# Two-stage softmax attention and a squared-ReLU MLP on one core: batch 0 in pieces, the first softmax transposed on VectorE, pv as small products for two quads

## Chip, core and metric

The program runs on one core of a Trainium2 chip. The time is the device time of one execution in microseconds; the time before is the median of three runs, 251.08 us (250.28 to 251.39). A core has five engines with a queue of instructions each, which they work off in order: TensorE (PE, matrix products; PEld is its loading of weights), VectorE (DVE), ScalarE (ACT), GpSimd (POOL) and SyncE (SP). They wait for one another by semaphores. Sixteen DMA engines move data between device memory (HBM) and the on-chip SBUF; SP's and ACT's DMAs go through hardware queues, POOL's through a software queue that can also convert f32 to bf16 on the way. PE writes to PSUM, eight banks of 2 KB per partition; ACT and DVE read it.

## What is computed

Shapes: 8 batches, 8 heads, 576 positions, head dimension 64; 32 packing queries p per head; the MLP has 512 inputs, 2048 hidden units and 512 outputs, on 4608 rows.

```python
def sm_attn(qq, kk, vv):
    s = scale * np.matmul(qq, kk.transpose(0, 1, 3, 2))
    s = s - np.max(s, axis=-1, keepdims=True)
    a = np.exp(s)
    a = a / (np.sum(a, axis=-1, keepdims=True) + 1e-09)
    return np.matmul(a, vv)
p_packed = sm_attn(p, k, v)
attn = sm_attn(q, p_packed, p_packed)
x = attn.transpose(0, 2, 1, 3).reshape(B * S, H * D)
h = x @ w_in
out = np.maximum(h, 0.0) ** 2 @ w_out
```

## The kernel before

Four heads of one batch make a quad (QH = 4), so each batch b has two quads, qd = 0 and 1. Four heads of 32 packing queries fill the 128 partitions. The kernel never forms x: it multiplies the packed result of the first attention by w_in (wp, "w" steps), and layer 1 is that product applied to the second softmax.

The order of all work is written out by hand in the string ORDER; each word is one step, and `run` walks the words, so the words give the order on every engine's queue. Digits name batch and quad, a letter after a colon the engine (v = DVE, a = ACT, p = POOL). The steps, for a quad:

- Lk, Lq, Lv: load k, q, v (`load1`), by POOL's queue, f32 to bf16. k and q lie as 128 partitions of 18 consecutive rows; v as 96 partitions (PS) of 6 rows (J). For batches in PAIRED (2 to 7) the q of quad 1 is loaded with its halves swapped, in two DMAs (`group`).
- kT, qT: DVE transposes in 32x32 blocks. P0, P1: p of batch 0 and 1, cast and transposed on DVE; p_f, their f32 source, is the first DMA of SP, in `setup`.
- s1: scores of p with k (`scores`, 16 products of 32x32 weights a quad), m1 their maximum (DVE), x1 the exponential with its sum (ACT), rd the reciprocal of the sum.
- eT, eo: the exponentials are transposed by PE, six products against the identity, and copied from PSUM (`st_e1T`, `st_e1T_out`). pv: 24 products with v (`st_pv`). pp: times the reciprocal. bd: DVE transpose of pp; pt, po: pp transposed by PE and copied.
- s2: scores of q with the packed result, t2 their transpose out of PSUM by DVE, m2 the maximum per query, sb the subtraction, x2 the exponential, su sum and reciprocal, a2 the scaling, aT the transpose to a2T.
- w0, w1 and W0, W1: the packed result times w_in, 512 of its columns at a time, and the copy of it to SBUF. Wi, Wo: loads of w_in and w_out in four pieces each.

Then, for each batch: h, layer 1 of one block of 128 hidden units (16 blocks) over half of the positions (b.half.block; batch 0 takes both halves in one step); r, the ReLU out of PSUM (ACT or DVE); q with dots, the square, written to gT (DVE). o tt.j: two of the 16 accumulating layer-2 products for the 128 output rows of tile tt; c: the copy of its result, and SP's stores. In time, layer 1 of batch b, layer 2 of the batch before and the attention of the batch after are woven together.

The Z words are products of zeros on PE into ps_idle (Z32 is 32 of them). PSUM is split by stages (STAGES): four banks stay with psa, in pairs, for all of the attention; the other four are first three "spare" banks and one for Z, then two pairs for batch 0's layer 1, then two for o and two "early", then two for o and two for h.

```python
STAGES = ((("spare", 3), ("idle", 1)), (("pair", 2),), (("pso", 2), ("early", 2)), (("psh", 2),))
```

## Time and profile before

| | |
|---|---|
| median of three runs | 251.08 us (250.28 to 251.39) |
| span of the profiled execution, first to last instruction | 248.6 us |
| first layer-1 product (h) begins | 23.15 us |
| first layer-2 product (o) begins | 37.3 us |
| last layer-2 product ends | 243.8 us |
| DMA, HBM read / written | 37.22 MB / 9.44 MB |
| PE's granted clock, mean | 0.995 |

The profile is of one execution. Busy times are the time in which an engine had an instruction at work; instructions of PE overlap, so a matmul's own duration is longer than the distance to the next one. "Releaser" is what ended an engine's wait. The costliest groups of the page (line, engine, operation, output<-input, shapes, count | busy us, mean ns | idle us before it):

```profile
L490 PE MATMUL ps_o<-w_out_bf,gT 128*128 128x512 bf16 x544 | 144.2, 379 | 2.0 <-issue 0.5
L444 ACT ACTIVATE r<-ps_h 128x288 bf16<-128x288 f32 (+1 forms) x181 | 73.1, 426 | 55.9 <-PE ps_h L438 47.5
L438 PE MATMUL ps_h<-a2T,wp 128*128 128x288 bf16 x512 | 91.9, 286 | 1.4 <-ACT r L444 1.4
...
L479 DVE TENSOR_TENSOR gT<-r 128x576 bf16<-128x576 bf16 x128 | 54.7, 448 | 5.2 <-ACT r L444 4.9
```

The first two lines of PE are layer 2 and layer 1; ACT's ReLUs wait for PE (47.5 us in all), not PE for them (1.4 us).

### The profile page before, as it was taken

The numbers are of one execution on the slowest core, as the hardware profiler recorded it, in microseconds if no ns is written. First come the engines' busy times: TensorE is split into PE (matmuls) and PEld (weight loads), VectorE is DVE, ScalarE is ACT, GpSimd is POOL, SyncE is SP. The second block draws the span as 40 slices with busy tenths as digits, with TensorE's granted clock in tenths as the row PEclk, the third lists the DMA queues.
The fourth block names the chain that finished last, engine by engine and source line by source line (L and its number), as shares of the span: only waits on it lengthen the run. The fifth ranks groups of instructions, "written<-read, shape, count | busy, mean of one in ns | idle before, by whom it ended". The sixth has DMA issues, their size and how long they took to land.

```text
span 248.6 us, 6041 instructions
## 1 busy us (share of the span) xinstructions
PE 237.1 (95%) x2415; PEld 132.2 (53%) x2447; DVE 194.2 (78%) x411; ACT 145.7 (59%) x316; POOL 45.8 (18%) x75
## 2 busy tenths in 40 slices
PE   8998899998999999999999999999999999999992
PEld 5655554465556554655456555655555555555540
DVE  1888899978988899979887998898897798644710
ACT  2346784476968748755764658676957555353100
POOL 8329634350401500033000230010000000000000
PEclk9999999999999999999999999999999999999997
DMA  6999999999791992269812794252121213211323
GB/s 112 203 207 205 206 197 209 197 142 259 161 171 64 157 211 45 46 93 187 185 42 45 135 130 122 64 90 56 42 45 42 45 42 82 49 42 44 70 63 82
DMA packets 23358, 28.52 MB, mean 115 GB/s; under 512 B 4257, under 2 KB 14753, under 8 KB 23329
## 3 DMA queue, kind: packets, MB, share of 16 engines
q0 software_dynamic: 16880, 18.55, 47.1%
q1 hardware_dynamic: 6288, 9.44, 15.0%
q8 instruction: 19, 0.31, 0.5%
q10 hardware_dynamic: 160, 0.13, 0.2%
q14 instruction: 11, 0.08, 0.1%
HBM read 37.22 MB, written 9.44 MB: 188 GB/s over the span
## 4 chain that ended last, share of the span: by engine, by line
PE 81%; DMA 10%; issue 2%; DVE 2%; POOL 2%; ACT 1%; SPq 0%; ACTq 0%; POOLq 0%
PE ps_o L490 48%; PE ps_h L438 24%; DMA v_b<-in_v_dram 4%; PE ps_wp L422 3%; PE ps_s L295 3%; DMA w_in_bf<-in_moe_w_in_dram 3%; DMA out_dram<-o_sb 3%; PE ps_e1T L339 1%; PE ps_pv L352 1%; POOL k_b L242 1%; DVE mx L387 1%; POOL d L391 0%; ACT r L444 0%; POOL q_b L242 0%; PE ps_ppT L372 0%
## 5 line engine op out<-in xcount | busy, mean ns | idle before, releaser
L490 PE MATMUL ps_o<-w_out_bf,gT 128*128 128x512 bf16 x544 | 144.2, 379 | 2.0 <-issue 0.5
L444 ACT ACTIVATE r<-ps_h 128x288 bf16<-128x288 f32 (+1 forms) x181 | 73.1, 426 | 55.9 <-PE ps_h L438 47.5
L438 PE MATMUL ps_h<-a2T,wp 128*128 128x288 bf16 x512 | 91.9, 286 | 1.4 <-ACT r L444 1.4
L490 PEld LDWEIGHTS <-gT 128*128 128x128 bf16 x576 | 54.9, 98 | 42.1 <-issue 3.3
L438 PEld LDWEIGHTS <-wp 128*128 128x128 bf16 x512 | 47.4, 98 | 44.4 <-issue 7.7
L479 DVE TENSOR_TENSOR gT<-r 128x576 bf16<-128x576 bf16 x128 | 54.7, 448 | 5.2 <-ACT r L444 4.9
L446 DVE TENSOR_SCALAR r<-ps_h 128x288 bf16<-128x288 f32 (+1 forms) x59 | 28.5, 484 | 20.0 <-PE ps_h L438 18.8
L332 ACT CAST wp<-ps_wp 128x1024 bf16<-128x1024 f32 x29 | 28.9, 1016 | 3.8 <-PE ps_wp L422 3.7
L332 ACT COPY o_sb<-ps_o 128x512 f32<-128x512 f32 x27 | 15.9, 588 | 10.8 <-PE ps_o L490 9.4
L321 ACT ACTIVATE e<-ps_s,nm 128x576 bf16<-128x576 f32 x16 | 11.8, 736 | 13.0 <-DVE nm L316 13.0
L233 POOL DMA_DIRECT2D v_b<-in_v_dram x16 | 11.1, 695 | 44.2 <-PE ps_pv L352 22.5
L279 DVE STREAM_TRANSPOSE kT<-k_b 128x576 uint32<-128x576 uint32 x16 | 15.0, 943 | 5.1 <-DMA k_b<-in_k_dram 5.1
L263 PE MATMUL ps_idle<-nought 128*128 128x288 bf16 x95 | 14.4, 304 | 1.1 <-DVE nought L178 1.1
L383 DVE STREAM_TRANSPOSE s<-ps_s 128x576 f32<-128x576 f32 x16 | 12.0, 767 | 2.4 <-PE ps_s L295 2.4
L401 DVE TENSOR_REDUCE sums<-e 128x18 f32<-128x576 f32 x16 | 11.9, 741 | 1.4 <-ACT e L396 1.3
L242 POOL DMA_DIRECT2D k_b<-in_k_dram x16 | 9.0, 562 | 21.4 <-DVE kT L279 12.5
L422 PE MATMUL ps_wp<-w_in_bf,ppT 64*32 64x512 bf16 x256 | 11.4, 382 | 0.8 <-DMA w_in_bf<-in_moe_w_in_dram 0.7
L316 DVE TENSOR_REDUCE nm<-ps_s 128x1 f32<-128x576 f32 x16 | 11.6, 739 | 0.6 <-PE ps_s L295 0.6
L285 DVE STREAM_TRANSPOSE qT<-q_b 128x576 uint32<-128x576 uint32 x16 | 12.0, 761 | 0.0
L387 DVE TENSOR_REDUCE mx<-s 128x18 f32<-128x576 f32 x16 | 11.9, 743 | 0.1
L396 ACT ACTIVATE e<-d 128x576 f32<-128x576 f32 x16 | 11.0, 685 | 1.6 <-DVE d L391 1.4
L263 PEld LDWEIGHTS <-nought 128*128 128x128 bf16 x95 | 9.2, 103 | 4.9 <-issue 1.2
(47 smaller groups left out, 153.0 us busy)
## 6 DMA issues: line engine op xcount, KB each, us to landing
out_dram<-o_sb SPq DMA_DIRECT2D x70, 128.0 KB, 2.8
k_b<-in_k_dram POOLq DMA_DIRECT2D x16, 288.0 KB, 8.1
v_b<-in_v_dram POOLq DMA_DIRECT2D x16, 288.0 KB, 7.4
q_b<-in_q_dram POOLq DMA_DIRECT2D x10, 288.0 KB, 7.2
w_in_bf<-in_moe_w_in_dram POOLq DMA_DIRECT2D x4, 512.0 KB, 12.5
w_out_bf<-in_moe_w_out_dram POOLq DMA_DIRECT2D x4, 512.0 KB, 13.8
q_b<-in_q_dram POOLq DMA_DIRECT2D x12, 144.0 KB, 3.9
p_b<-in_p_dram POOLq DMA_DIRECT2D x1, 192.0 KB, 11.5
```

The lines of the kernel that those rows point to most:

```text
L263: self.nc.tensor.matmul(ps[:, :HALF], lhsT=self.nought[:, :P], rhs=self.nought, start=True, stop=True)
L279: return self.nc.vector.transpose(t["kT"][:].rearrange("p (j l a) e -> p a j l e", j=J, a=3).bitcast(U32).rearrange("p a j l e -> p a j (l ...
L285: return self.nc.vector.transpose(t["qT"][:].rearrange("p s e -> p (s e)").bitcast(U32), t["q"][:].rearrange("p t d -> p (t d)").bitcast(U32))
L332: engine.copy(out, x)
L383: nc.vector.transpose(s2[:].rearrange("p (a t) i -> p a (t i)", a=2), t["ps_s2"][:, :, :HALF])
L387: self.nc.vector.tensor_reduce(out=t["mx"], in_=t["s2"], op=ALU.max, axis=AX.X)
L422: self.nc.tensor.matmul(ps[NP * h:NP * h + NP, c, :], lhsT=t["ppT"][D * c:D * c + D, NP * g:NP * g + NP], rhs=self.w_in_bf[D * c:D * c + D ...
L438: self.nc.tensor.matmul(ps, lhsT=t["wp"][:, fb // n, fb % n * P:(fb % n + 1) * P], rhs=t["a2T"][:, hf * HALF:(hf + 1) * HALF], start=(qd = ...
L444: engine.activation(r, ps, ACT.Relu)
L446: engine.tensor_scalar_max(r, ps, 0.0)
L479: (engine or self.nc.vector).tensor_tensor(out=out, in0=r, in1=r, op=ALU.mult)
L490: self.nc.tensor.matmul(self.o[tt], lhsT=self.gT[:, fb, a:a + P], rhs=self.w_out_bf[:, fb, :], start=(i == 0), stop=(i == self.NFB - 1))
```

## The change

The new kernel has another ORDER throughout and these changed steps.

- k of batch 0 is loaded as f32 by SP's queue into the still unused last two blocks of gT, and cast to bf16 in two halves, one on DVE and one on ACT (ka, kb). p_f is no longer loaded in `setup` but by the word pf, between the two k's.
- v lies like k and q, 18 rows to a partition. The exponentials of the first softmax are transposed by DVE in 32x32 blocks (eo); PE's transposes and their copies are gone. pv is 18 rounds of products with 32 rows and 32 columns; from batch 1 on both quads run in one step, on different tiles of the array (8 products a round, 144 in all), as do rd, pp, bd, pt, po and s2.
- PAIRED begins with batch 1; q is loaded whole, and v of quad 1 with its halves swapped.
- The second softmax of batch 0 runs in two parts, positions 0 to 319 and 320 to 575 (tA, mA, sA, xA, uA, aA, TA and tB to TB), and so do layer 1, ReLU and square of batch 0 (PARTS).
- w_in is loaded as four quarters of 256 columns and two pieces of 512; wp of batch 0 has two quarter steps (wa, wb) ahead of w1.
- POOL does more of the subtractions (sb), scalings (a2) and some squares of batch 0. Z32 at the start is gone.
- The second stage of PSUM is two banks "x" and two "y" for everything behind the first layer-1 step.

```diff
-PAIRED = range(2, 8)
+PAIRED = range(1, 8)
+PARTS = {False: ((0, HALF), (HALF, S)), True: ((0, 320), (320, S))}
 ORDER = """
-Lk00 Lk01 Lq00 kT00 P0 Z32 s100 kT01 I m100 x100 Z5 s101 m101 x101 Lq01 P1 Z7 eT00 Lv00 eo00:a Lk10 Z10 pv00 rd00
-qT00 rd01 qT01 pp00:v bd00 eT01 kT10 Lv01 Z3 s200 Wi00 Wi01 pt00 eo01:a Lk11 Z5 pv01 s110 pp01:a t200 pt01 Wi10 bd01
...
+Lk00 I pf Lk01 Lq01 Lv00 Lq00 Lv01 kb00:v ka00:a Wi11 P1 P0 Wi01 kT00 Wi10 kb01:a s100 ka01:v Wi00 m100 Wi20 kT01 x100
+qT01 Z15 s101 Wi21 eo00 rd00 m101 Z2 pv00 x101 Lk11 pp00:v qT00 bd00 Z7 pt00 rd01 eo01 s200 Lv11 po00:v pv01 tA00 tB00
+pp01:a mA00 Lk10 bd01 Z5 pt01 mB00 s201 po01:a sA00:v sB00:p tB01 Wo0 xB00 tA01 xA00 mB01 Z10 wb00 Wo2 mA01 Wb00:a
+wb01 uB00 sA01:p uA00 Wb01:a Z4 wa01 Lv10 aB00:v xA01 aA00:v wa00 sB01:p Wa01:a uA01 Wa00:a TA00 aA01:p xB01 TB00 TA01
+Lq10 uB01 Z16 h0.0.0 h0.0.1 r0.0.0:a h0.0.10 r0.0.1:v h0.0.3 aB01:p r0.0.10:a h0.0.8 q0.0.0:v r0.0.3:a h0.0.9 h0.0.2
...
-    STAGES = ((("spare", 3), ("idle", 1)), (("pair", 2),), (("pso", 2), ("early", 2)), (("psh", 2),))
+    STAGES = ((("spare", 3), ("idle", 1)), (("x", 2), ("y", 2)))
...
+    def bank(self, pool, name):
+
+        return self.banks(pool).tile([P, 512], F32, name=name, tag="t")
...
+    def load_w_in(self, n, c):
+        f0, f1 = ((0, 256), (256, 512), (512, 1024))[n]
...
     def load1(self, b, qd, n):
+        s = getattr(self, n)[b, qd * QH:(qd + 1) * QH].rearrange("h (l t) d -> (h l) t d", t=T)
+        x = self.ld.tile([P, T, D], BF16, name=f"{n}_b")
...
+        if (n, b) == ("k", 0):
+
+            f = self.gT[:, self.NFB - 2:, :].rearrange("p f s -> p (f s)").bitcast(F32)[:, qd * T * D:(qd + 1) * T * D]
+            t["f"] = f.rearrange("p (t d) -> p t d", d=D)
+            self.nc.sync.dma_start(t["f"], s)
+        elif n == "v" and self.group(b, qd, 0):
+            n2 = P // 2
+            self.nc.gpsimd.dma_start(x[:n2], s[n2:])
+            self.nc.gpsimd.dma_start(x[n2:], s[:n2])
         else:
+            self.nc.gpsimd.dma_start(x, s)
...
+    def st_cast(self, t, n, engine):
+        x = slice(n * T // 2, (n + 1) * T // 2)
+        self.copy(engine, t["k"][:, x, :], t["f"][:, x, :])
...
-    def st_e1T(self, t, b):
-        ps = self.bank16(b, "ps_e1T")[:PS, :J * P].rearrange("p (j c) -> p j c", c=P)
-        for j in range(J):
-            self.nc.tensor.transpose(ps[:, j, :], t["e1"][:, j * PS:(j + 1) * PS], self.ident)
-        t["ps_e1T"] = ps
-
-    def st_e1T_out(self, t, engine):
-        t["e1T"] = self.tp.tile([PS, J, P], BF16, name="e1T")
-        self.copy(engine, t["e1T"], t["ps_e1T"])
+    def st_e1T(self, t):
+
+        t["e1T"] = self.tp.tile([P, T // 2, NP, 2], BF16, name="e1T")
+        self.nc.vector.transpose(t["e1T"][:].rearrange("p t i e -> p (t i e)").bitcast(U32), t["e1"][:].bitcast(U32))
...
+    def st_pv(self, b, *qds):
+
+        ps = self.bank32(b, "ps_pv", len(qds))
+        for j in range(T):
+            for i, qd in enumerate(qds):
+                t = self.att[b, qd]
+                t["ps_pv"] = ps
+                for h in range(QH):
+                    r, c = NP * self.group(b, qd, h), NP * h
+                    self.nc.tensor.matmul(ps[c:c + NP, i, :D], lhsT=t["e1T"][r:r + NP, j // 2, :, j % 2],
+                                          rhs=t["v"][r:r + NP, j, :], start=(j == 0), stop=(j == T - 1))
...
+    def span(self, hf):
+
+        s0, s1 = (0, S) if hf is None else PARTS[True][hf]
+        return slice(s0 // NP, s1 // NP)
...
+    def st_sub2(self, t, engine, hf=None):
+        x = self.span(hf)
+        d2 = self.new(t, self.tp, "d2", [P, T, NP], F32)
+        n = x.stop - x.start
+        engine.tensor_tensor(out=d2[:, x], in0=t["s2"][:, x], in1=t["mx"][:, x].unsqueeze(2).to_broadcast([P, n, NP]),
+                             op=ALU.subtract)
...
+    WP = {"0": (0, 512), "a": (0, 256), "b": (256, 512), "1": (512, 1024)}
...
+    def step_h(self, engine, b, hf, fb):
+
+        s0, s1 = PARTS[b == 0][hf]
+        ps = self.ph[b, hf, fb] = self.bank("y" if b or fb % 2 else "x", "ps_h")
+        self.layer1(ps[:, :s1 - s0], b, fb, s0, s1)
...
+        elif word == "pf":
+            self.nc.sync.dma_start(self.p_f, self.packed(0, 2 * self.NQ))
```

## The prediction

> **What bounds the kernel now.** I read the engine totals first, then busy time by stretch, then the chain of waits, then the timeline of the first 36 us, then the groups with their shapes kept apart.
>
> ```profile
> span 248.6 us, 6041 instructions
> PE 237.1 (95%) x2415; PEld 132.2 (53%) x2447; DVE 194.2 (78%) x411; ACT 145.7 (59%) x316; POOL 45.8 (18%) x75
> ...
> PE 81%; DMA 10%; issue 2%; DVE 2%; POOL 2%; ACT 1%; SPq 0%; ACTq 0%; POOLq 0%
> ```
>
> TensorE (PE) is busy 95% of the span and carries 81% of the chain. Its own count includes 14.4 us of ps_idle matmuls (the Z words), so the start needs a look of its own.
>
> ```profile
> 23.00:37.70 14.70, 13.43 (x192) 8.00 (x186) 12.60 (x28) 10.83 (x18) 8.18 (x13) 1.00 1.34 202
> 37.70:60.00 22.30, 21.26 (x239) 10.72 (x242) 20.07 (x41) 12.69 (x26) 8.12 (x11) 1.00 1.12 199
> 60.00:235.00 175.00, 173.26 (x1680) 96.63 (x1706) 144.82 (x312) 111.44 (x255) 16.82 (x29) 1.00 0.47 91
> ```
>
> Columns: stretch, its length, then busy PE, weight loads, DVE, ACT, POOL. From 60 us on PE lacks 1.7 us in 175, and 32 of the 576 second-layer matmuls have no record, so it is full. Three places can move the end: when the first layer-1 matmul (ps_h) runs, at 23.15 us; what PE has to do from there to 243.8; and its holes, 2.3 us between 23 and 60 (1.27 + 1.04). The last 4.8 us (copy and store of tile 35) stay. So 23.15 + 220.7 + 4.8 = 248.6. The median of the runs, 251.08, is 2.5 above this span; I carry that over.
>
> **Part 1: less on PE per batch.** Taken away: six transposes a quad (eT) and a pv of 24 products with 96 rows. Added: one pv of 144 products with 32 rows for both quads.
>
> ```profile
> 31.81 0.29 PE ps_pv L352 x24
> ...
> 33.25 0.62 PE ps_s L295 x16
> ```
> ```profile
> 99.18 0.63 PE ps_s L295 x32
> ...
> 130.61 0.67 PE ps_e1T L339 x12
> ```
>
> These are pieces of the chain: start, length, what. One transpose is 0.67/12 = 56 ns; after 23.15 there are 13 quads of six, 4.4 us. A quad's pv is 0.29 us, 14 of them 4.1 us; some pairs stand side by side and share the change of tile shape, and the chain's shares (e1T 1.4%, pv 1.3%) give 6.7 us for both together. I take 8.0. The new pv is 18 rounds of eight. A round's price: today 24 products (last one 193 ns long) fill 0.36 us, (0.36 - 0.19)/23 = 7.3 ns each, 29 ns for a round of four. Does a round of eight cost the same? The scores say so: 16 small products take 0.62 us and 32 take 0.63, because the second quad uses other tiles of the array. So a new pv is 18 x 30 ns and 0.22 us for going into small tiles and out, 0.76 us; 7 times 5.3 us. Net **-2.7 us**. Bounds: rounds at 29 ns and 8.5 us removed, -3.3; the two quads one after the other, 18 x 58 ns, 8.9 us, against 6.7 removed, +2.2. I stay near the scores' row, which is the same form of product.
>
> The Trainium skill, "TensorE: Matmul & The Clock Gate", section "Wait — 56ns, not 53.3ns?", speaks against this part: starts never come closer than about 25 ns. By it a pv would take 3.6 us. The 7.3 ns above disagree; it stays as a rival of small chance.
>
> **Part 2: what moves to VectorE (DVE).** The transposes become 16 DVE instructions like a2T's:
>
> ```profile
> L415 DVE STREAM_TRANSPOSE a2T<-a 128x288 uint32<-128x288 uint32 x16 | 7.0, 457 | 0.2
> L391 POOL TENSOR_TENSOR d<-s,mx 128x576 f32<-128x576 f32 x3 | 3.6, 1191 | 7.6 <-DVE mx L387 7.6
> ```
>
> +7.3 us. The new order also gives DVE 6 more wp copies (7.3), 6 more o_sb copies (4.1), some 23 more relus of 288 (10.4), wider pp (about +1.8) and reciprocals (+1). It takes from it e1T copies (3.9), 11.5 subtractions (8.7), 6.5 scalings (5.2), 5 squares (2.2), smaller relus in batch 0 (0.9) and ppT copies (1.0). Net about +10, DVE 204 us. ACT falls to about 120; POOL gets 32 tensor operations where it had 6, about 37 us. In 60 to 180 us DVE was 87% busy (105 of 120 us), so 5% more makes 92%. On average that hides under PE. But DVE and POOL get in each other's way here:
>
> ```profile
> 42.59 1.26 POOL L391 TENSOR_TENSOR d<-s,mx 128x576 f32<-128x576 f32 x1
> ```
> ```profile
> 42.76 1.77 DVE L479 TENSOR_TENSOR gT<-r 128x576 bf16<-128x576 bf16 x2
> ```
>
> Two squares take 1.77 us instead of 0.90: the first waits until POOL's subtraction ends at 43.85. With four POOL operations a batch (4.7 us of some 27) and 16 squares, 2.8 squares a batch run into one and lose some 0.5 us: 1.4 us, 5%, so DVE stands at 97%. A late square or relu holds the two ps_h banks and then PE. I take **+0.7 us** for all later batches; bounds 0 (each wait falls into slack) and +4 (half of 7 x 1.4 shows).
>
> The Trainium skill, "SBUF — State Buffer", section "Who interferes with whom", makes this a lock: a DVE instruction with two SBUF inputs and a POOL instruction that reads SBUF exclude each other entirely. The trace agrees with 1.77 for 0.90; by that rule each meeting costs the whole rest, as counted.
>
> **Part 3: the start.** Today p_f lands before 3 us, the first scores run at 7.05, the second v lands at 14.4 (seventh transfer of 1.4 us each, saturated), the last w_in piece at 26.8.
>
> ```profile
> 23.15 1.15 PE L438 MATMUL ps_h<-a2T,wp 128*128 128x288 bf16 x8
> ...
> 26.82 0.41 PE L422 MATMUL ps_wp<-w_in_bf,ppT 64*32 64x512 bf16 x7 [0.70 <-DMA w_in_bf<-in_moe_w_in_dram]
> ```
>
> After: both k of batch 0 come as f32 through SP's queue (first issue 0.74, first packet 1.85 as p_f had). A 4,608-byte packet is not shown; stores of 1,024 and 2,048 bytes take 74 and 131 ns, which gives about 270; the cast packet that reads as much takes 192. Eight packets an engine: k00 lands at 4.7 with the 0.6 us to a semaphore (today 5.6). Then on DVE half a cast 0.4 (not shown; between the 0.25 of p_b's 128 elements and the 0.8 of a 576-element scaling), the four p instructions 1.0 (they were half hidden), kT 0.95: scores at 7.1, no gain. The second k shares the engines with POOL's loads. Stores and loads that overlap at 63 to 64.5 us go packet for packet (86 to 94), so 8 x (0.27 + 0.19) us from 5.0: it lands at 9.2. Its cast (ka01) stands on DVE ahead of the first row maximum, which moves from 8.00 to 9.6. Z32 is gone, so Z15 runs unwarmed (the first 32 today take 168 ns each, later ones 123) and holds the second scores to about 12.
>
> From there DVE's queue sets the pace, with durations from today's rows less the 0.07 us by which neighbours overlap: second maximum 12.9 to 13.6, pp 14.1, qT and first bd 14.9, second e1T 15.4, second pv on PE 15.7 to 16.3 (v landed near 13: six transfers instead of seven), second bd 17.05. Then the softmax in pieces of 320 and 256, each at 320/576 or 256/576 of its row: transposes, maxima and the one DVE subtraction to 19.3, sums 20.3, scalings 21.4 with one meeting with POOL, last sum 22.0, POOL's scaling 22.7, transpose 23.1. First ps_h at **23.2: no gain**. The second half, from second bd to ps_h, shrinks from 7.9 us to 6.1, and the later first half eats it. w_in does not bind: four quarters at 1.5 us after v put the first half there by 19, the second by 24. Bounds: 22 (k in 192 ns packets, nothing shared) and 28.5 (p_f's 32 small packets an engine alternate with loads of 192 ns, 6.7 us, and k01 queues behind them).
>
> Part 3b, the ramp. Before PE reaches o0.0 it has 9.3 us of work (32 half-width h 7.85, two wp steps, s11). DVE has 8 relus, 10 squares, a wp copy (1.2), two kT (1.9) and remainders of the softmax, 10 us by slots, and 1.7 for meetings with five POOL squares (not shown; the 1.16 of 576 elements gives 1.0 to 1.3): PE gets there near 35, with 2.6 us of holes plus nothing for w_in, against 2.3 today. **+0.3** (-1 to +3).
>
> **Sum:** 0 - 2.7 + 0.7 + 0.3 = -1.7: span 246.9, time **249.4**. v in one 4,608-byte run per partition, q unswapped and v swapped instead, merged pp, ppT: nothing, as PE is full over them; a pv fetch of 288 instructions at once is the uncovered one (inside the bound of part 1).
>
> **Rivals.** (a) The second k is late: SP's queue gets less than its turn while POOL's loads saturate the engines. For it: the first store of today, issued at 50.6 into such a stretch, landed 7.2 us later, against 2.8 in the median. Against: it alternated evenly at 63 us. Until 10 the unwarmed Z15 covers it, then each microsecond delays ps_h by one; from 11.7 on it eats the whole gain. At the 28.5 bound 249.4 + 5.3 = 254.7; half way 252. (b) DVE with POOL's lock becomes the bound from 40 to 180 us: +4 instead of 0.7, 252.7. Against: at 88% from 60 to 120 us it leaves PE full today. It decides once PE's holes pass 2.4 us. (c) The quads' pv do not overlap: 249.4 + 4 = 253.4. (d) As the skill's 25 ns, 7 x 2.8 us more: 269. (e) The pieces work better than I walk: k early, ps_h at 21.5 to 22, ramp without holes (-2) and DVE covered: 246. For it: from second bd on the chain is shorter by 1.8 us already. (f) The order leaves PE as full as it was and nothing shows: 251.
>
> **Chances.** A measurement tells 0.5%, 1.26 us, from no change: faster is below 249.8, slower above 252.3. Forecast 0.42 (its own range 247.3 to 251.3: faster 0.26, same 0.16); (a) 0.15 slower; (b) 0.12 (slower 0.08, same 0.04); (c) 0.06 and (d) 0.01 slower; (e) 0.22 faster; (f) 0.02 same. Faster 0.48, same 0.22, slower 0.30. Range 245.3 to 253.8: it leaves out the best of (e), the worst of (a), and (d).
>
> **What would show it.** pv of both quads near 0.76 us on PE; no e1T on PE; the DVE wait at ka01 and where k01 lands; the first ps_h at 22 to 25; PE idle under 3 us up to o0.0 and under 1.5 from 60 on; squares of 1 us or more beside POOL operations. I am wrong if ps_h starts before 21.5 or after 25, if pv takes over 1.2 us, or if PE has holes in 60 to 180 us.

## The result, and the profile after

The changed kernel takes 265.39 us (median of 4 runs, 264.28 to 265.94) where the kernel before, run beside it, takes 251.24 (4 runs): ratio 1.0543, 95% interval 1.0483 to 1.0602. It is slower by 14 us; the forecast was 249.4, in a range from 245.3 to 253.8. The profiled execution has a span of 262.5 us at a clock of 1.00, 13.9 more than the 248.6 of before.

The page of the changed kernel, engine totals, the instruction queue among the DMA queues, and the chain by engine:

```profile
span 262.5 us, 7413 instructions
PE 237.1 (90%) x3099; PEld 128.5 (49%) x3099; DVE 210.3 (80%) x445; ACT 124.5 (47%) x280; POOL 73.9 (28%) x102
...
q8 instruction: 24, 0.39, 0.6%
...
PE 65%; DVE 25%; DMA 4%; issue 3%; ACT 1%; SPq 0%; POOL 0%; ACTq 0%; DVEq 0%; POOLq 0%
```

PE's busy time is given as 237.1 us, as before, although its idle products (ps_idle) fell from 14.4 to 9.7 us: the change took nothing off PE. (The records of before lack 32 products, so its true figure is somewhat higher.) DVE carries 25% of the chain where it had 2%, and "issue", time in which nothing in the profile is waited for, 3% (2% before). The packets of PE's instructions (q8, 16,384 bytes each) were 19 before and are 24.

Busy time by stretch, in the stretches shown of before (stretch, length, PE, weight loads, DVE, ACT, POOL, clock, DMA):

```profile
23.00:37.70 14.70, 12.10 (x110) 7.57 (x108) 13.78 (x30) 10.51 (x28) 10.93 (x14) 1.00 1.17 208
37.70:60.00 22.30, 18.77 (x308) 8.46 (x309) 16.85 (x33) 9.24 (x18) 10.11 (x14) 1.00 0.95 148
60.00:235.00 175.00, 171.88 (x2296) 93.28 (x2295) 155.09 (x326) 94.44 (x214) 41.22 (x52) 1.00 0.48 94
```

PE loses in every stretch. DVE's 155.1 us in the third are 89% of it, against 83% before (144.8); POOL has 41 us for 17.

Take the time from each product's start to the next: the usual time of its form is its slot, what is over is a hole. That gives the bill. The first ps_h runs at 26.3 instead of 23.15 us (+3.2). The slots from there on add up to 217.1 instead of 216.4 us (+0.7). Holes from there to 60 us are 7.7 instead of 4.2 (+3.5), and after 60 us 6.3, where before shows none but its 32 unrecorded matmuls (+6.3). Together 13.7 of 13.9. Three kinds of places make it up. The timeline of the start, the rows where an engine waited long:

```profile
7.38 0.23 DVE L208 TENSOR_SCALAR p_b<-p_f 128x128 bf16<-128x128 f32 x1 [2.64 <-DMA p_f<-in_p_dram]
...
10.24 0.46 DVE L338 CAST k_b<-gT 128x576 bf16<-128x576 f32 x1 [1.31 <-DMA gT<-in_k_dram]
...
20.56 0.69 PE L303 MATMUL ps_s<-qT,ppd 32*32 32x320 bf16 x16 [2.27 <-issue]
```

DVE waits 2.64 us for p_f (in this execution; other runs with the same start do not show it, see e1) and 1.31 for the second k; and PE stands 2.27 us in front of the second quad's second scores although their weight load could begin at 18.36. The same kind of stop comes in batch 1; the timeline of PE there:

```profile
44.62 1.34 PE L367 MATMUL ps_pv<-v_b,e1T 32*32 32x64 bf16 x144
45.90 1.90 PE L529 MATMUL ps_o<-w_out_bf,gT 128*128 128x512 bf16 x8
...
48.27 0.56 PE L303 MATMUL ps_s<-qT,ppd 32*32 32x288 bf16 x19
51.08 0.44 PE L303 MATMUL ps_s<-qT,ppd 32*32 32x288 bf16 x13 [2.25 <-issue]
```

pv of both quads takes 1.34 us, not 0.76, and the scores stop after 19 of 32 products. The first sixteen have read all the tiles (qT, ppd of both quads) that the rest read, so no operand can be late there. The third kind, all engines near 193 us:

```profile
192.96 2.09 DVE L518 TENSOR_TENSOR gT<-r 128x576 bf16<-128x576 bf16 x3
...
193.18 1.18 POOL L455 TENSOR_TENSOR a<-e,rs 128x576 bf16<-128x576 f32 x1 [2.62 <-ACT r L496]
...
194.73 0.61 PE L529 MATMUL ps_o<-w_out_bf,gT 128*128 128x512 bf16 x2 [0.78 <-DVE gT L518]
```

Three squares fill 2.09 us instead of some 1.3 while POOL's scaling runs from 193.18 to 194.36, and PE waits 0.78 us for the last. The page's squares take 515 ns each on the mean, 448 before, but the 515 mixes three shapes. Those of 576 elements, the only shape of before, take 489:

```profile
L518 DVE TENSOR_TENSOR gT<-r 128x576 bf16<-128x576 bf16 x112 | 53.0, 489 | 3.1 <-ACT r L496 2.1
```

### The profile page after: what moved, and what is told of

Read it like the earlier page. It is cut to its first block, busy times and chain, and to the rows that moved or that the text cites. A ratio compares the mean times of both kernels' runs of the same rounds, so it can differ in the third digit from the quotient of the medians.

```text
span 262.5 us, 7413 instructions
## 1 busy us (share of the span) xinstructions
PE 237.1 (90%) x3099; PEld 128.5 (49%) x3099; DVE 210.3 (80%) x445; ACT 124.5 (47%) x280; POOL 73.9 (28%) x102
## 4 chain that ended last, share of the span: by engine, by line
PE 65%; DVE 25%; DMA 4%; issue 3%; ACT 1%; SPq 0%; POOL 0%; ACTq 0%; DVEq 0%; POOLq 0%
PE ps_o L529 37%; PE ps_h L491 18%; DVE gT L518 7%; PE ps_s L303 4%; PE ps_pv L367 4%; DMA p_f<-in_p_dram 2%; DVE wp L338 2%; DVE sums L447 2%; DVE mx L429 2%; DVE r L498 2%; DMA out_dram<-o_sb 2%; DVE s L416 2%; PE ps_wp L475 2%; PE ps_idle L267 1%; DVE qT L293 1%
## 5 line engine op out<-in xcount | busy, mean ns | idle before, releaser
L496 ACT ACTIVATE r<-ps_h 128x288 bf16<-128x288 f32 (+2 forms) x172 | 66.2, 412 | 76.4 <-PE ps_h L491 72.8
L491 PE MATMUL ps_h<-a2T,wp 128*128 128x288 bf16 (+2 forms) x512 | 91.5, 287 | 3.6 <-DVE a2T L464 1.4
L491 PEld LDWEIGHTS <-wp 128*128 128x128 bf16 x512 | 48.1, 98 | 50.2 <-issue 11.2
L518 DVE TENSOR_TENSOR gT<-r 128x576 bf16<-128x576 bf16 (+2 forms) x123 | 61.4, 515 | 3.2 <-ACT r L496 2.1
L498 DVE TENSOR_SCALAR r<-ps_h 128x288 bf16<-128x288 f32 (+2 forms) x84 | 37.2, 452 | 13.8 <-PE ps_h L491 12.9
L435 POOL TENSOR_TENSOR d<-s,mx 128x576 f32<-128x576 f32 (+2 forms) x16 | 18.6, 1166 | 56.5 <-DVE mx L429 56.5
L336 ACT CAST wp<-ps_wp 128x1024 bf16<-128x1024 f32 (+1 forms) x25 | 23.2, 955 | 8.9 <-PE ps_wp L475 8.8
L455 POOL TENSOR_TENSOR a<-e,rs 128x576 bf16<-128x576 f32 (+2 forms) x11 | 11.9, 1081 | 14.9 <-DVE rs L449 11.2
L329 ACT ACTIVATE e<-ps_s,nm 128x576 bf16<-128x576 f32 x16 | 11.8, 743 | 4.2 <-DVE nm L324 4.2
L324 DVE TENSOR_REDUCE nm<-ps_s 128x1 f32<-128x576 f32 x16 | 11.7, 748 | 1.3 <-PE ps_s L303 1.3
L441 ACT ACTIVATE e<-d 128x576 f32<-128x576 f32 (+2 forms) x18 | 11.0, 635 | 2.6 <-POOL d L435 2.6
L447 DVE TENSOR_REDUCE sums<-e 128x18 f32<-128x576 f32 (+2 forms) x18 | 11.9, 663 | 0.2 <-ACT e L441 0.2
L429 DVE TENSOR_REDUCE mx<-s 128x18 f32<-128x576 f32 (+2 forms) x18 | 11.6, 660 | 0.0
## 6 DMA issues: line engine op xcount, KB each, us to landing
w_in_bf<-in_moe_w_in_dram POOLq DMA_DIRECT2D x4, 256.0 KB, 11.8
```

The costliest lines, as they stand in the source:

```text
L336: engine.copy(out, x)
L429: self.nc.vector.tensor_reduce(out=mx[:, x], in_=t["s2"][:, x], op=ALU.max, axis=AX.X)
L435: engine.tensor_tensor(out=d2[:, x], in0=t["s2"][:, x], in1=t["mx"][:, x].unsqueeze(2).to_broadcast([P, n, NP]), op=ALU.subtract)
L447: nc.vector.reduce_sum(out=sums[:, x], in_=t["e2"][:, x], axis=AX.X)
L491: self.nc.tensor.matmul(ps, lhsT=t["wp"][:, fb // n, fb % n * P:(fb % n + 1) * P], rhs=t["a2T"][:, s0:s1], start=(qd == 0), stop=(qd == se ...
L496: engine.activation(r, ps, ACT.Relu)
```

## The experiments

The theory I set out to test: (A) PE's instructions come too slowly for the bursts of pv, and pv itself is limited by instructions; (B) POOL's tensor operations shut out DVE's two-input ones. The rivals: DVE's load, the start's transfers, the order of the work. Times of before are 251.4 to 251.7 in these runs.

| run | time, us | ratio to before, 95% interval |
| --- | --- | --- |
| changed kernel | 265.39 | 1.0543 (1.0483 to 1.0602) |
| e1 p_f first | 264.85 | 1.0546 (1.0503 to 1.0589) |
| e2 half of pv | 256.12 | 1.0199 (1.0151 to 1.0246) |
| e3 pv with 32 columns | 262.81 | a single run |
| e4 pv in two halves | 267.15 | 1.0582 (1.0504 to 1.0660) |
| e5 160 instructions more | 271.79 | 1.0774 (1.0703 to 1.0845) |
| e6 p_f first, fewer idle products | 265.31 | 1.0527 (1.0466 to 1.0588) |
| e7 subtractions on DVE | 269.95 | 1.0727 (1.0667 to 1.0788) |
| e8 relus on ACT | 263.55 | 1.0482 (1.0408 to 1.0556) |
| e9 eight POOL operations on DVE | 261.82 | 1.0394 (1.0330 to 1.0459) |
| e10 quads apart, 4 o_sb | 261.72 | 1.0380 (1.0309 to 1.0451) |
| e11 all repairs | 259.52 | 1.0296 (1.0231 to 1.0362) |
| e13 all repairs, relus on ACT | 259.52 | 1.0328 (1.0287 to 1.0369) |
| e16 without 13 subtractions | 262.23 | 1.0397 (1.0342 to 1.0453) |
| e12 before, 24 steps on POOL | 261.46 | 1.0383 (1.0322 to 1.0445) |
| e14 before, no step on POOL | 253.63 | 1.0100 (1.0070 to 1.0131) |
| e15 before, batch 1's steps on DVE | 251.54 | 0.9992 (0.9962 to 1.0022) |

### What a pv product costs, and half of pv

Half of pv:

```diff
-        for j in range(T):
+        for j in range(0, T, 2):
...
-                                        ..., stop=(j == T - 1))
+                                        ..., stop=(j == T - 2))
```

> Only every second round of the pv products is issued (9 of 18), so half of pv is left out; 72 products a batch instead of 144, in batch 0 36 instead of 72 for each quad. Theory (a round of eight costs 64 ns, and the burst of 288 instructions, products and their weight loads, runs PE's instruction supply dry): pv falls from 1.16-1.34 to about 0.65 us for each of 7 batches (-4.2), the stalls put down to issue at 18.4 (2.2 us) and 48.5 (2.4 us) are gone or under 0.5, PE's instruction fetches fall from 24 to about 20; time about 257 to 258. Rival (the two stalls come from something else, a late operand or a full DMA queue): pv falls the same, the two stalls of over 2 us stay; time about 261.5.

Products of 32 columns:

```diff
-    matmul(ps[c:c + NP, i, :D], lhsT=..., rhs=t["v"][r:r + NP, j, :], ...)
+    matmul(ps[c:c + NP, i, :NP], lhsT=..., rhs=t["v"][r:r + NP, j, :NP], ...)
```

> Each pv product streams 32 columns of v instead of 64, so the other half of pv's columns is left out; as many products and weight loads as before. Theory (PE takes in small products and their weight loads at about 4 ns an instruction, 8 ns a product): unchanged, 144 products in 1.16 us or more, 8 ns each. Rival (the array or PSUM limits: the quads' tiles do not overlap, and a product occupies something for its columns): 32 columns take half, about 4 to 5 ns a product, 0.6 to 0.7 us for 144. Time 265 by the first, 261 by the second.

The timeline of e3, PE, pv of batch 1 and the scores behind it:

```profile
43.30 1.32 PE L367 MATMUL ps_pv<-v_b,e1T 32*32 32x32 bf16 x144
...
49.50 0.44 PE L303 MATMUL ps_s<-qT,ppd 32*32 32x288 bf16 x13 [2.01 <-issue]
```

144 products take 1.32 us with half the columns and 1.34 with all: 7.96 and 8.05 ns from start to start. So the columns do not set the price, and neither do the tiles: one quad alone (72 products, four tiles) starts a product every 7.8 to 8.0 ns too. What is common is two instructions a product, a weight load and a matmul, some 4 ns each. Which of the two sets it was not tried. The rows of the weights do not matter either: the pv of before, with 96 rows, has starts 7.2 to 7.7 ns apart. The scores do better than 8 ns only in appearance: eight of them start close together and then wait for 288 columns.

In e2, pv falls to 0.75 us (72 products) as both sides expected, the fetches fall to 19, the stop behind pv of batch 1 is gone and the first ps_h comes at 24.7. The time fell by 9.3 us, to 256.12, a little below the theory's 257 to 258. The profiled execution, 257.73 us, shows a new wait (ACT, then PE):

```profile
61.73 0.58 ACT L336 COPY o_sb<-ps_o 128x512 f32<-128x512 f32 x1 [2.15 <-DMA out_dram<-o_sb]
```
```profile
62.37 0.59 PE L529 MATMUL ps_o<-w_out_bf,gT 128*128 128x512 bf16 x2 [1.81 <-ACT o_sb L336]
```

The fourth o_sb copy must wait until the first store, issued among the loads, has left its buffer. In the changed kernel the stop at 48.5 had covered this: ACT waited 0.41 us there. Between these two profiles, then, the stop of 2.4 us costs only some 0.5 net.

### The stops: a burst, a place, or the supply of instructions

pv in two halves of nine rounds, two PE steps apart (batch 1 shown):

```diff
- o3.0 pv1 o3.1 pp1 Lk21 o1.1 qT10
+ o3.0 pv1 o3.1 Lk21 o1.1 pw1 pp1 qT10
```

> In batches 1 to 7 the pv products are issued in two halves of 9 rounds with two PE steps (0.25 to 0.43 us each) between them; batch 0 is left as it is. Each half goes into and out of small tiles by itself, 7 x 0.19 us more. Theory (the burst outruns the instruction supply): the stall of 2.4 us behind pv of batch 1 is cut to under 1.2, that of 0.6 behind pv of batch 5 goes; time 265.4 - 1.8 + 1.3 = 264.9. Rival (a stall that has nothing to do with the burst): both stay, and the time is 266.7 by the tile changes and a later pp.

It came out as the rival said: the stop in s21 is still there (2.6 us, at 49.0). The packets of the instruction queue tell why. Places were counted in PE's weight loads and matmuls, in order. Packets are 256 instructions long, and the stops fall on places 449 and 1217, three times 256 apart, in e1, e3 and e4 as well as in the changed kernel. In e4 the piece from 961 to 1216 was entered at 44.7 us and run dry at 49.0 all the same: two steps are only 0.9 us. So the next run moves the places instead of the burst:

```diff
- qT01 Z15 s101
+ qT01 Z11 Y84 s101
...
+    def small(self, n):
+        ps = self.banks("idle").tile([P, 512], F32, name="ps_idle")
+        for i in range(n):
+            r = c = NP * (i % 4)
+            self.nc.tensor.matmul(ps[c:c + NP, :NP], lhsT=self.nought[r:r + NP, :NP],
+                                  rhs=self.nought[r:r + NP, :NP], start=True, stop=True)
```

> Z15 is replaced by 11 of its products and 84 tiny ones (32x32 on a diagonal tile), about as long together; every later PE instruction stands 160 places further on. Theory (PE takes its instructions in pieces of 256; a piece is asked for when PE enters the piece before it and is there 2.4 us after its packet starts, 3 to 4 us after the request while the loads fill the DMA engines until about 72 us and about 1 us later on; a stall comes where one piece is run through in less): worked out from the instruction times of the changed kernel with boundaries moved by 160, the stalls at 18.4, 48.5 and 179.6 us are under 0.3, and new ones of 2 to 4 us stand at 66 to 70 (scores and pv of batch 2) and of 0.5 to 2 near 130; first ps_h near 25, time 264 to 267. Rival (these stalls belong to their place: the burst itself, an operand, the DMA engines): the stalls of 2.2 to 2.4 us behind pv01 and behind pv of batch 1 stay where they are, none appears at 66 to 70; time 265.5 to 266.

The timeline of e5, PE, batches 2 and 4:

```profile
68.33 1.32 PE L375 MATMUL ps_pv<-v_b,e1T 32*32 32x64 bf16 x141
71.77 0.21 PE L375 MATMUL ps_pv<-v_b,e1T 32*32 32x64 bf16 x3 [2.12 <-issue]
...
129.20 1.33 PE L375 MATMUL ps_pv<-v_b,e1T 32*32 32x64 bf16 x142
132.95 0.23 PE L375 MATMUL ps_pv<-v_b,e1T 32*32 32x64 bf16 x2 [2.41 <-issue]
```

The stops at 18.4, 48.5 and 179.6 are gone; two new ones stand in the middle of pv, three and two products before its end, where no data can be the reason, at 69.5 and 130.3 as forecast. That settles it: the supply of instructions. Places and packets fit one rule at all of these stops. From the trace's records, us: when PE enters a piece of 256, when the next piece's packet starts, PE's last instruction before the stop (a weight load in the first row, products in the others), its first product after it, and the time from the packet to that.

```
kernel    enters    packet    last     first    packet to first
changed   14.58     18.13     18.4     20.56    2.43
changed   44.99     48.68     48.5     51.08    2.40
e5        68.39     69.17     69.5     71.77    2.60
e5       129.27    130.73    130.3    132.95    2.22
e6        12.77     16.34     17.0     18.75    2.41
```

A piece is asked for when PE enters the one before it; its packet starts 2 to 5 us later while the loads fill the DMA engines (in the changed kernel up to 73 us) and mostly within 1.5 us in the rest of the kernel; 2.2 to 2.6 us after its start PE can use it. The entry is known to about a microsecond only: from 100 us on, seven packets of the changed kernel start 0.2 to 1.3 us before it. A piece with most of a pv in it is run through in less. The Trainium skill, "Runtime: NRT & Kernel Launch", section "Instruction fetch mechanics", has the blocks of 256 and calls the cost of crossing one mostly hidden. The 24 packets of 16,384 bytes agree; that it stays hidden does not: 2.2 to 2.6 us here. The time of e5 was higher than I said, 271.8 for 264 to 267: beside the two stops the wait for o_sb came back (1.84 us at 61.3), and the products of batch 0 took 12 ns. The trace shows one thing more: from 132.2 us, near the end of the stop that begins at 130.3, to 139.0 PE's granted clock is 0.50, and products of 512 columns start 427 ns apart instead of 216. Half of those 6 us, some 3 us, is lost there (an estimate). The changed kernel's own two stops, 2.3 and 2.4 us long, have no such stretch behind them. Nor did the first ps_h come near 25: it is at 26.2, as the second k landed at 11.35 and the stop at 18.4 was not the only thing that held it.

The quads' pv apart, each a burst of 144 instructions, and a fourth o_sb buffer (batch 1 shown):

```diff
- eo11 q0.1.2:p o1.0 x110 ... eo10 Lq20 o3.0 pv1
+ eo11 q0.1.2:p o1.0 pv11 x110 ... eo10 Lq20 o3.0 pv10
...
-        self.op = pool("op", 3)
+        self.op = pool("op", 4)
```

> In batches 1 to 7 each quad's pv is a word of its own, the first one right after its own e1T, the second where pv of both stands now, 1.5 to 4 us later; o_sb gets 4 buffers instead of 3. Theory (a burst of 288 PE instructions runs through a piece of 256 before the next piece is there; and a pair of quads saves nothing, 8.05 ns a product as one quad alone): two bursts of 144 cost 0.74 to 0.76 us each plus 0.19 for another change of tile shape, +1.8 us in all; the stall at 48.5 falls from 2.4 to under 0.8, that at 179.6 goes, and with a fourth o_sb buffer no wait for a store takes its place near 61: time 265.4 + 1.8 - 2.9 = 264.3. Rival (the pieces are late whatever the burst): both stalls stay, 267.2.

The timeline of e10, PE, batch 1:

```profile
42.87 0.75 PE L362 MATMUL ps_pv<-v_b,e1T 32*32 32x64 bf16 x72
43.55 1.90 PE L524 MATMUL ps_o<-w_out_bf,gT 128*128 128x512 bf16 x8
45.38 0.75 PE L362 MATMUL ps_pv<-v_b,e1T 32*32 32x64 bf16 x72
...
48.43 0.79 PE L293 MATMUL ps_s<-qT,ppd 32*32 32x288 bf16 x32
```

All 32 scores run through, nothing waits at 61 or at 179, and the time is 261.72, 3.7 us less than the changed kernel and 2.6 less than I expected; the two edits were not run apart. What is left after 60 us is 5.0 instead of 6.3. Only the stop in batch 0 stays (2.4 us at 18.0): there the bursts follow too closely.

### The start

```diff
- Lk00 I pf Lk01
+ pf Lk00 I Lk01
```

> The p_f transfer is issued ahead of k00 on SP's queue; nothing else changes. Theory (p_f late sets the start): today k00 lands at 4.19 us and DVE then waits 2.64 us for p_f, until 7.38. With p_f first that wait is under 0.3 us, kT of quad 0 starts near 5.7 instead of 7.43 and the first scores run near 6.5 instead of 8.98, Z15 ends that much earlier, and the first ps_h moves from 26.3 to about 24.3; time about 263.4. Rival (the second k, landing at 10.24, and the wait of 1.31 us for it set the start): p_f's move only changes places with k01, the second scores stay at 13.2 us and the first ps_h at 26 or later; time 265.4 +- 0.5.

The rival was nearer. The wait for p_f is gone, but now k00 lands at 6.21 instead of 4.19 us, behind p_f; the first scores run at 8.30 instead of 8.98, the first ps_h at 25.8 instead of 26.3, and the time does not differ from the changed kernel's. The wait of 2.64 us belongs to that one execution: in five runs that leave the start as it is (e7 to e10 and e16) p_f is there with k00, DVE does not wait for it, and the first scores run at 6.6 to 6.9, yet the first ps_h comes at 25.6 to 26.8. What p_f's place does move is the second k: it lands at 9.27 with p_f first, at 10.2 to 11.3 in those five. The PE timeline of e1 shows what holds the second scores here:

```profile
9.38 3.28 PE L267 MATMUL ps_idle<-nought 128*128 128x288 bf16 x15
12.59 0.69 PE L303 MATMUL ps_s<-kT,pT 32*32 32x288 bf16 x16
```

The second scores follow right behind the idle products; their kT was ready at 11.08. So next also `Z15` cut to `Z4`:

> p_f first on SP's queue, and the 15 idle products ahead of the second scores cut to 4. Theory (in the first 13 us the idle products hold the second scores: kT of quad 1 is ready at 11.1 us, the scores of quad 1 run at 12.6 with p_f first and at 13.2 without): the second scores run at 11.2 to 11.4, the second maximum at 12, and the first ps_h comes 1.0 to 1.5 us earlier than the 25.8 of p_f alone, as far as the stall of 2.4 us ahead of the second quad's second scores lets it: 24.4 to 24.8; time about 263.5. Rival (DVE's queue sets the pace, or the colder clock lengthens the scores): the second maximum stays behind qT and e1T on DVE at 12.5 or later and the first ps_h at 25.5; time 265.

The second scores run at 10.4 and the first ps_h at 24.2, a little earlier than expected, as the second k landed at 8.50; the time, 265.3 where 263.5 was expected, does not show it. The stop moved with the 22 instructions that fell away (11 products and their weight loads): it now comes after 11 of the 16 products of s201 instead of ahead of the first, which agrees with the count. Other stops grew (1.0 us at 151.9, in pv of batch 5).

### POOL against DVE

> The 13 subtractions of batches 1 to 7 that run on POOL go to VectorE, as 11.5 of them did before; POOL keeps 19 tensor operations. Theory (POOL's operations shut out DVE's two-input ones; 123 squares now take 515 ns on the mean against 448): the squares fall to about 480, PE's holes after 60 us fall from 6.4 to about 4; time about 263. Rival (DVE is overloaded, and each piece of its work counts): 13 x 0.75 = 9.8 us more on DVE, less 4 us of squares, PE's holes after 60 us grow to 8 or more; time 267.

```diff
- sb11:p  sb21:p  sb20:p  ... (13 words)
+ sb11:v  sb21:v  sb20:v  ...
```

The rival won: the holes after 60 us grow to 11.8. The mean of the squares falls to 497 ns; those of 576 elements fall from 489 to 469.

```diff
- r2.0.0:v  r2.0.10:v  ... (every second of the 54 words of batches 2 to 6)
+ r2.0.0:a  r2.0.10:a  ...
```

> Every second of the 54 relus that DVE does in batches 2 to 6 goes to ScalarE, 27 in all: DVE 12 us less, ACT 11 us more, at the same places in the order. Theory (DVE's load and queue make the holes after 60 us): PE's holes after 60 us fall from 6.4 to 4 or less, time about 263. Rival (lock, instruction supply and single late links make them): the holes stay at 6 to 7; time 265.4 +- 0.7.

DVE falls to 200.9 us, squares stay at 515 ns, and the holes after 60 us stay where they were, most to within 0.02 us (85.0, 162.1, 163.7, 193.8). So DVE's load as a whole is not what makes them; the time is inconclusive.

```diff
- q0.0.5:p  q0.1.0:p  q0.0.3:p  q0.0.7:p  q0.1.2:p  a220:p  sb50:p  a261:p
+ q0.0.5:v  q0.1.0:v  q0.0.3:v  q0.0.7:v  q0.1.2:v  a220:v  sb50:v  a261:v
```

> Eight of POOL's tensor operations go to VectorE: the five squares of batch 0 and the three steps of batches 2, 5 and 6 beside which a square on DVE stood still ahead of a hole on PE (scaling at 83.9, subtraction at 160, scaling at 193.2 us). Theory (POOL's lock makes these holes): a POOL square takes 1.04 to 1.35 us and keeps DVE's squares out for most of it, DVE itself needs 0.45 to 0.5, so DVE gains time although it takes work over; the holes at 30.8 (1.53), 37.3 (0.95), 39.7 (0.59), 85.2 (0.86), 162.1 (0.47), 163.7 (0.59) and 193.7 (0.94), 5.9 us in all, fall to under 2.5; profiled span 259 against 262.5, time about 262. Rival (DVE is simply full there): the holes stay or grow, as they did with the 13 subtractions on DVE; time 266 or more.

The groups of squares with shapes kept apart, the changed kernel, then e9:

```profile
L518 POOL TENSOR_TENSOR gT<-r 128x640 bf16<-128x640 bf16 x3 | 3.9, 1294 | 1.3 <-DVE r L498 1.2
L518 DVE TENSOR_TENSOR gT<-r 128x640 bf16<-128x640 bf16 x5 | 3.8, 778 | 0.1
L518 DVE TENSOR_TENSOR gT<-r 128x512 bf16<-128x512 bf16 x6 | 4.6, 783 | 0.0
```
```profile
L518 DVE TENSOR_TENSOR gT<-r 128x640 bf16<-128x640 bf16 x8 | 3.7, 479 | 0.1
L518 DVE TENSOR_TENSOR gT<-r 128x512 bf16<-128x512 bf16 x8 | 3.1, 406 | 0.0
```

Five squares of 640 on DVE beside three on POOL take DVE 3.8 us; all eight on DVE take 3.7. Of the squares of 512, six beside two on POOL take 4.6; all eight take 3.1. POOL's help there was worth nothing, and it cost latency: of the holes of batch 0 the ones of 0.95 and 0.59 are gone and that of 1.53 is 0.87. The time falls by 3.6 us, as the theory said. After 60 us it is not so clear: 0.47 at 162 is gone and 0.94 at 193.7 is 0.67, but 0.86 at 85 became 1.23, where the scaling itself is now in DVE's queue ahead of the transpose that PE needs, and the sum stays at 6.2. The holes named come to 3.4, not under 2.5. To take POOL's work away without giving it to DVE, e16 leaves out the row maximum's subtraction where POOL does it:

```diff
     def st_sub2(self, t, engine, hf=None):
+        if engine == "none":
+            t["d2"] = t["s2"]
+            return
```

> The changed kernel without the 13 subtractions that POOL does in batches 1 to 7: the exponential there reads the scores themselves, so the row maximum is not taken off. Neither POOL nor DVE does them; the quads' softmax chain is 1.2 us shorter each. Theory (POOL's lock makes the holes after 60 us): squares fall from 515 to about 485 ns, the holes from 6.3 to 3.5 or less; time about 262.5. Rival (the order itself: squares, copies and transposes stand on DVE just ahead of the PE step that needs them, and anything in front shows): squares fall too, the holes at 85.2, 163.7, 179.6, 193.7 and 223.8 stay, 5 or more in all; time 264 to 265.

The holes after 60 us fall from 6.3 to 4.2, between the two forecasts. They do so place by place: those beside subtractions (162.1, 163.7, 218.0, 223.8) are gone, those beside scalings, which are still on POOL, stay with their lengths (0.86 at 84.9, 0.94 at 192.0). Squares of 576 elements take 469 ns. That speaks for POOL's operations as the cause at these places; the chain that is 1.2 us shorter was changed at the same time, so the lock alone is not shown for them.

### All repairs together

> All repairs together: p_f first, 4 idle products instead of 15 ahead of the second scores, the eight POOL operations on DVE, quads apart, four o_sb buffers. If the parts add up: profiled span 262.5 - 2.1 (first ps_h at 24.2) - 3.4 (lock) - 2.9 + 1.8 (bursts) = 255.9, time about 258.5, which is still 7 us over the kernel before. If each hole is only covered by the next one: 262 or more. Under 251 would need pv cheaper than two e1T transposes and pv of before, which 8 ns a product excludes.

The parts nearly add up: span 256.3 (255.9 expected), time 259.52 (258.5). First ps_h 24.4, holes to 60 us 2.8, after it 4.9. It is 5.9 us better than the changed kernel and still 8 over the kernel before. The relus on ACT on top of it:

> All repairs of the stack, and 27 of DVE's 54 relus of batches 2 to 6 on ScalarE as in the relu run. Theory (once the bursts are cut and eight POOL operations are gone, DVE's late links make what is left of the holes after 60 us, 1.24 at 78.7, 0.59 at 157.9, 0.67 at 187.4 and smaller ones, 4.9 in all): 11 us less on DVE halve them; time 257, span 254. Rival (POOL's lock at single places and links of the softmax chain make them, whatever DVE's load): the holes stay at 4 to 5, time 259.5 +- 0.7.

Again nothing: the four largest holes after 60 us, 1.23, 0.59, 0.66 and 0.32, are those of e11. So the rest does not follow DVE's load as a whole.

### The kernel before, with and without POOL

```diff
- sb20:v  a220:v  ... (24 words of batches 2 to 7)
+ sb20:p  a220:p  ...
```

> The kernel before with the 12 subtractions and 12 scalings of batches 2 to 7 on POOL instead of VectorE; nothing else. DVE gets 18.6 us less work, POOL 28 more. Theory (POOL and DVE shut each other out, and the longer POOL step, 1.19 and 1.16 us against 0.75 and 0.80, lengthens the softmax chain): squares rise from 448 to over 500 ns, PE's holes after 60 us rise by 2 to 5 us; time 253 to 256. Rival (less work on DVE is what counts): 251 or less.

Slower by 10 us, far more than expected, but mostly for another reason. Squares rise to 506 ns, and two holes make 7.6 us: 2.4 for a store at 58.7, and 5.2 at 69, where DVE waits for a k that POOL could issue only behind its own subtractions at 63.7 and 65.7 (DVE timeline of e12):

```profile
73.27 0.94 DVE L279 STREAM_TRANSPOSE kT<-k_b 128x576 uint32<-128x576 uint32 x1 [7.70 <-DMA k_b<-in_k_dram]
```

From 73.2 us, shortly before that hole ends, to 80.0 the granted clock is 0.50, some 2.8 us more (an estimate: half of the time from 74.4 on). So this run does not price the lock. The opposite one, all six of before's POOL steps on DVE and 4 o_sb buffers:

> The kernel before with its 6 POOL tensor operations (3 subtractions, 3 scalings) on VectorE and a fourth o_sb buffer; nothing else. It tells the lock apart from the order of POOL's loads, which the run of the kernel before with 24 more POOL operations mixed. Theory (lock): the two squares that took 1.77 us beside a subtraction at 42.6 take 0.9, the squares' mean falls from 448 to under 440 ns, and the holes between 23 and 60 us shrink by 0.5 to 1 us; time 250 to 250.8. Rival (DVE's load): 4.7 us more on DVE, holes as before or 1 us larger; 251.4 to 252.4.

Slower by 1%, against both forecasts. Squares fall to 440 ns, the pair of 1.77 us is 0.82, but the first ps_h runs at 27.0: in batch 0 DVE is the chain, and a wait for its kT holds PE (PE timeline of e14):

```profile
25.95 1.15 PE L295 MATMUL ps_s<-kT,pT 32*32 32x288 bf16 x16 [2.75 <-DVE kT L279]
```

From 25.4 to 28.8 the granted clock is 0.50. There a POOL step is worth its place, lock or not. With only the three steps of batch 1 on DVE:

> The kernel before with POOL's three operations of batch 0 kept (they shorten VectorE's chain to the first ps_h) and its three of batch 1 on VectorE, where the squares run; a fourth o_sb buffer. Theory (lock where squares run, and a store that an o_sb buffer waits for at 58 us): the first ps_h stays at 23.2, the holes from there to 60 us fall from 3.0 to about 2, the squares' mean to 440 ns; time 250.2 to 250.8, the first that would be under the kernel before. Rival (DVE's extra 2.3 us eats it): 251.4 +- 0.5, no difference.

0.9992, no difference, with squares at 440 ns; in its profile the first ps_h came at 24.6, and PE still waited 1.6 us at 51 for a copy to o_sb, which stood on ACT behind two late exponentials. POOL's three steps of batch 1 cost the kernel before nothing that can be measured, and no run is measurably faster than it.

## Why the prediction was wrong

In the terms of the sum, forecast and measured: the start 0 and +3.2, PE's work -2.7 and +0.7, the ramp +0.3 and +3.5, the later holes +0.7 and +6.3; together -1.7 and +13.7. Every term was off, so no single step carries the miss.

**PE's work (part 1), the step that failed first.** The price of a product was read nearly rightly, 7.3 ns for the 8.05 measured. The step that failed was to give a round of eight the price of a round of four. "Does a round of eight cost the same? The scores say so": they do not. Scores are held apart by their 288 columns; pv products have 64 and follow the instructions, 8 ns each, 64 ns a round, whatever the number of tiles. The term was 7 x 0.76 = 5.3 us. Measured are 143 starts of 8.05 ns and the same 0.22 us for the change of tiles, 1.37 us a batch, 9.6 in all, against the 8.0 taken away: +1.6 instead of -2.7 (the slots of all PE products say +0.7). Rival (c) had nearly the size, 58 ns a round, for another reason. Rival (d) is out: the 25 ns between starts that the Trainium skill gives in "TensorE: Matmul & The Clock Gate", section "Wait — 56ns, not 53.3ns?", stand against 8.05.

**What was costed at nothing.** The sum said that "a pv fetch of 288 instructions at once" was uncovered and lay inside part 1's bound. It was outside: 2.2 us at 18.4, 2.4 at 48.5, 0.6 at 179.6. This is the mechanism I named and did not price. The trace of before held a part of what was needed, its 19 packets of 16,384 bytes and a longest pv burst of 96 instructions, but none of its stops.

**The start (part 3).** Forecast 23.2, measured 26.3. k00 landed at 4.19 (4.7 forecast), k01 at 10.24 (9.2), kT took 0.77 instead of 0.95. In the profiled execution DVE waited for p_f and the unwarmed idle products held the second scores to 13.2 (12 forecast). In the five runs with the same start the idle products are over by 11.2 to 11.7, and the second scores wait until 12.2 to 13.1 for kT of k01, which landed 1 to 2 us later than forecast. So rival (a), the late second k, was right about what holds them. Behind it comes the instruction stop ahead of s201, 2.3 us (1.8 to 2.5 in the five), which the walk did not have. How the 3.1 us divide between the two was not measured: with p_f first and four idle products k01 landed at 8.5 to 9.3 and the stop shrank to 1.5 to 1.8, and the first ps_h came at 24.2 to 25.0 (e6, e11, e13).

**The ramp (3b).** +0.3 was forecast with bounds -1 to +3; it was +3.5. In it are the stop at 48.5, 2.4, and 3.1 in three holes beside POOL's squares. I had given the meetings of squares 1.7 us. DVE's eleven squares beside POOL's took 3.8 us more than at e9's lengths (5 x 0.30 and 6 x 0.38), and PE's part of it I let go under.

**Steady state (part 2).** The load came out nearly as reckoned (DVE 210.3 for 204, POOL's 32 operations 36.5 us for 37). The error is in "on average that hides under PE". The loss does not spread: it sits where one square, transpose or copy stands just ahead of the PE step that needs it. +0.7, at most +4, became 6.3. Of these, 0.6 is the instruction stop at 179.6, and 2.1 go when POOL's 13 subtractions are left out (e16). What makes the rest, over 3 us, is not shown: e9 took three operations from POOL at such places and the sum stayed at 6.2. Rival (b) had the size nearer, +4. Its first half, a DVE that is full, does not hold: 9.4 us less on DVE in e8 and 8.4 in e13 leave the large holes as they are. Its second half, POOL's lock, is borne out for the squares of batch 0 (e9) and only likely after 60 us.

**What stays open.** After all repairs the span is 7.7 us over before's: 1.2 at the start, 2.0 of PE slots (0.7, and 7 x 0.19 for the extra changes of tile shape), 4.9 of holes after 60 us, less 1.4 of holes up to 60; 1.0 is not placed. The largest of the holes stand where a scaling or a wp copy is late. Whether another order of the same words would close them was not tried.

The conditions that I set for being wrong were all met: ps_h after 25, pv of 1.34 us, holes between 60 and 180.

## What to carry to other kernels

Price small products by instructions as well as by columns and tiles: a form with few columns (pv) is not priced by a row with many (scores), even where the operands look alike. Count the PE instructions of a burst against the pieces in which they arrive, and keep dense bursts apart; a stop in the middle of products with the same operands, put down to "issue", is the sign, and adding harmless instructions ahead of it moves it. Work handed to POOL pays where DVE is itself the chain, and costs where DVE's two-input operations stand just ahead of a PE step; only a run with the operation at that place moved tells which.

## What the runs showed of the hardware

- In bursts of 72 or 144, a 32x32 product with its weight load starts every 7.6 to 8.05 ns, with 32 or 64 columns and on four or eight tiles alike; at the start of e5, where idle products of 288 columns start 240 ns apart instead of 122, 12 to 12.8 ns.
- PE's instructions come in packets of 16,384 bytes, one piece of 256 ahead. From the packet's start to use are 2.2 to 2.6 us, and while the loads run (up to 73 us) the packet starts 2 to 5 us after PE enters the piece before.
- A stop can hide a later one: without the 2.4 us at 48.5, a copy waited 2.0 to 2.2 us for an o_sb buffer whose store had been issued among the loads (e2, e5).
- Five squares on DVE beside three on POOL took DVE as long (3.8 us) as all eight alone (3.7).
- From about a microsecond before the end of PE stops of 2.6 us (e5) and 5.2 us (e12) the granted clock was 0.50 for 6.8 us, and of one of 2.8 us (e14) for 3.4; in the changed kernel, with stops of 2.3 and 2.4 us, it stayed at 1.00 up to the last product.
